# A wide weight conversion, a held first unit and held token-row weights in an RWKV-6 and MLP-mixer kernel

## The chip, the cores and the metric

One core of one Trainium2 chip. The metric is the device time of one execution in microseconds (us).

## The reference

```
attention:  state = 0
            for t: y[t] = r[t] . (state + u*k[t] (x) v[t]);  state = w[t]*state + k[t] (x) v[t]
            r,k,v,w: (4 batches, 8 heads, 768 tokens, 48), float32
mixer:      x = y as (4, 768, 384)
            u = x + (relu(x^T w_tok1) w_tok2)^T          w_tok1 (768,256), w_tok2 (256,768)
            out = u + relu(u w_ch1) w_ch2                w_ch1 (384,1536), w_ch2 (1536,384)
```

The four mixer weights arrive as 64-bit floats. The kernel loads their bits and makes 32-bit floats of them on VectorE.

## The kernel before

Twelve attention **units** (three for each batch, 256 tokens each) go through six levels: a product (`gram`) on TensorE, a **join** on VectorE that multiplies r and k by decays, and a pick of the product into a weight tile `at`. The mixer of batch b runs woven with the units of batch b+1. The profile names TensorE's products by their result: `h_ps` for the token products, `z_ps` for the products with `w_ch1`, `q_ps` for those with `w_ch2` (in the first part of batch 0 these are one long sum, also called `h_ps`, the "down product"). The framework puts each engine's instructions in an order of its own by estimated readiness, and an instruction that waited held its engine: in the trace of the kernel before, VectorE ran nothing in the 1.01 us before 200.14 us, for which L358, a row product shown below, waited for its load. A dependency of class NoSync only fixes which of two instructions of one engine is issued first. It added no wait: in experiment 10, where it ties each VectorE step of the conversion to the one before, the second mask step starts 0.33 us after the first, which takes 0.42; untied, in the kernel before, mask steps start 0.336 apart.

The conversion, two pieces of 128x512 a call, their steps alternating:

```
bits64 = [t[:, ts(i, 2 * PIECE)] for t in (scratch, spare) for i in range(2)]
...
def convert(pair, first):
    steps = []
    for n, (dst, src) in enumerate(pair):
        d64 = bits64[(first + n) % 4]
        sp.dma_start(d64..., src)
        ...
        steps.append([
            dve: e     = top & 0x7FF0                  # exponent
            act: power = Relu(8*e + rebias)
            dve: m     = hi & 0xFFFFF | 0x100000       # mantissa
            dve: mf    = lo * 2**-32 + m
            dve: mf    = mf * 2**-20 * power
            dve: dst   = hi & 0x80000000 | mf ])       # sign
    for both in zip(*steps):
        for f in both:
            f()
```

(The steps are abridged to one line each.) From unit 6 on, the weight of a token for itself and for its successor is made by rows on VectorE and then placed:

```
def row(c):
    ...
    dve.tensor_mul(rr, rr, k.unsqueeze(1).to_broadcast([128, 2, DM]))       # L357
    dve.tensor_mul(rr[:, 0], rr[:, 0], u_rows)                              # L358
    dve.tensor_reduce(out=sums[0][:, c], in_=..., op=ALU.add)               # L359
def place():  ...  dve.copy_predicated(out=weights_at[i % 3]..., ...)       # L370
...
return [(0.3, lambda: row(0)), (0.3, lambda: row(1)), (0.2, lambda: (place(), load_near(i + 1)))]
```

and unit i's products stand beside the levels of unit i+1 in this program order:

```
return [(1.0, begin[1]), tokens, one(carry, rest[0]), update, one(before, rest[1]), row0, one(within, rest[2]),
        *loads, row1, *rest[3:], place]
```

## Time and profile before

| | before |
|---|---|
| time, median of 6 runs | 609.95 us (608.86 to 610.78) |
| span of the profiled run | 607.9 us |
| TensorE busy | 578.5 us, 95% |
| VectorE busy | 362.6 us, 60%, in 685 instructions |
| ScalarE busy | 180.1 us, 30% |

TensorE's busy time is near the span, yet "busy" also counts products that run at half rate (from 227.59 us fourteen `q_ps` take 4.78 us, where the fastest steady rate, 0.1625 each, gives 2.3). The prediction therefore compares each window with the work in it at the fastest steady rate. I call the difference the **ledger's loss**, and use it throughout.

### The profile page before, as it was taken

To read this page: it belongs to the slowest core of one execution; us is meant where nothing else is said; L and a number is where in the kernel's file an instruction comes from. 1 tells how busy PE (TensorE), PEld (TensorE's weight loads), DVE (VectorE), ACT (ScalarE), POOL (GpSimd) and SP (SyncE) were. 2 spreads that over 40 slices of the span, in tenths; PEclk is the share of its full clock that TensorE was granted. 3 is DMA by queue.
4 is the path that set the end of the run, shared out by engine and by line. 5 is a ranking of instruction groups with operands and counts; after the bars stand their busy time and mean duration, and the time that the engine had idled before them with its cause. 6 is when DMAs were issued, how large, how long until landed. Compare 5 with 4: busy or idle time off the path is not lost.

```text
span 607.9 us, 18977 instructions
## 1 busy us (share of the span) xinstructions
PE 578.5 (95%) x8596; PEld 493.5 (81%) x8596; DVE 362.6 (60%) x685; ACT 180.1 (30%) x440; POOL 7.2 (1%) x32
## 2 busy tenths in 40 slices
PE   3889789999999989999999999999999999999997
PEld 2777467876988877689989897789899886898987
DVE  5888889998786998876545463526253432040403
ACT  6154655530433313143132222232212311303020
POOL 4000000000000000000000000000000000000000
PEclk9999779999999998999999999999999999999999
DMA  8326554630335364532112100000000000000000
GB/s 340 121 81 215 153 175 156 208 96 27 82 108 136 93 165 135 146 105 51 56 29 76 32 28 27 2 1 2 29 2 28 1 28 1 0 14 13 27 2 26
DMA packets 22976, 45.85 MB, mean 75 GB/s; under 512 B 2512, under 2 KB 14928, under 8 KB 22896
## 3 DMA queue, kind: packets, MB, share of 16 engines
q1 hardware_dynamic: 22752, 44.64, 23.6%
q8 instruction: 67, 1.10, 0.8%
q14 instruction: 13, 0.11, 0.1%
q10 hardware_dynamic: 144, 0.00, 0.0%
HBM read 39.91 MB, written 4.72 MB: 73 GB/s over the span
## 4 chain that ended last, share of the span: by engine, by line
PE 78%; DVE 15%; issue 2%; ACT 2%; DMA 2%; SPq 0%; DVEq 0%; ACTq 0%
PE z_ps L533 26%; PE q_ps L567 24%; PE gram L276 7%; PE h_ps L506 5%; PE h_ps L513 3%; PE h_ps L543 3%; PE kv_ps L413 2%; PE y_ps L468 2%; PE gram L403 2%; DVE rk L317 2%; PE y_ps L455 2%; DVE wch L192 1%; DVE sums L359 1%; DVE at L292 1%; PE gram L270 1%
## 5 line engine op out<-in xcount | busy, mean ns | idle before, releaser
L533 PE MATMUL z_ps<-xT,wch 128*128 128x256 f32 x864 | 195.6, 382 | 0.1
L533 PEld LDWEIGHTS z_ps<-xT,wch 128*128 128x128 f32 x864 | 161.0, 190 | 22.3 <-ACT z L535 1.4
L535 ACT ACTIVATE z<-z_ps 128x256 f32<-128x256 f32 x144 | 55.2, 383 | 167.3 <-PE z_ps L533 158.3
L567 PE MATMUL q_ps<-wch,z 128*128 128x192 f32 x528 | 97.5, 334 | 0.7 <-DVE o L589 0.7
L567 PEld LDWEIGHTS q_ps<-wch,z 128*128 128x128 f32 x528 | 88.3, 194 | 2.4 <-DVE o L589 1.0
L567 PE MATMUL q_ps<-scratch,z 128*128 128x192 f32 x396 | 70.2, 329 | 0.0
L276 PE MATMUL gram<-rk 48*64 48x32 f32 x3072 | 65.0, 239 | 4.4 <-DVE at L292 1.7
L276 PEld LDWEIGHTS gram<-rk 48*64 48x64 f32 x3072 | 60.6, 158 | 10.5 <-issue 3.8
L567 PEld LDWEIGHTS q_ps<-scratch,z 128*128 128x128 f32 x396 | 64.5, 190 | 0.6
L317 DVE TENSOR_TENSOR rk<-rk,w 112x1024 f32<-112x1024 f32 x27 | 32.8, 1222 | 30.5 <-PE gram L276 26.8
L317 DVE TENSOR_TENSOR rk<-rk,decay 112x1024 f32<-112x1024 f32 x27 | 33.0, 1222 | 27.1 <-PE gram L276 16.7
L559 DVE TENSOR_TENSOR z<-z 128x768 f32<-128x768 f32 x11 | 10.5, 956 | 61.0 <-ACT z L535 61.0
L506 PE MATMUL h_ps<-x,wtok 128*128 128x384 f32 x96 | 39.9, 561 | 1.8 <-ACT x L474 1.8
L513 PE MATMUL h_ps<-h,wtok 128*128 128x384 f32 x96 | 35.3, 492 | 0.0
L300 ACT COPY at<-gram 16x256 f32<-16x256 f32 x48 | 17.4, 364 | 58.5 <-PE gram L276 57.3
L292 DVE COPY_PREDICATED at<-mask,gram 128x512 f32<-128x512 uint8 x36 | 32.3, 897 | 0.0
L506 PEld LDWEIGHTS h_ps<-x,wtok 128*128 128x128 f32 x96 | 19.9, 220 | 13.1 <-issue 3.0
L515 DVE TENSOR_TENSOR x<-x,h_ps 128x384 f32<-128x384 f32 x24 | 13.3, 554 | 27.4 <-PE h_ps L513 27.3
L513 PEld LDWEIGHTS h_ps<-h,wtok 128*128 128x128 f32 x96 | 16.5, 190 | 9.5 <-ACT h L508 2.6
L287 ACT COPY at<-gram 32x256 f32<-32x256 f32 x48 | 17.4, 363 | 15.1 <-PE gram L270 14.6
L404 ACT COPY kT<-gram 128x512 f32<-128x512 f32 x24 | 14.1, 586 | 26.4 <-PE gram L403 26.2
L436 DVE TENSOR_TENSOR state<-state,kv_ps 128x192 f32<-128x192 f32 x30 | 10.7, 357 | 18.5 <-PE kv_ps L413 18.1
(90 smaller groups left out, 551.0 us busy)
## 6 DMA issues: line engine op xcount, KB each, us to landing
rk<-in_rkw_dram SPq DMA_DIRECT2D x36, 192.0 KB, 3.5
scratch<-in_w_ch_dram SPq DMA_DIRECT2D x10, 512.0 KB, 4.3
vt<-in_v_dram SPq DMA_DIRECT2D x12, 384.0 KB, 4.2
out_dram<-o SPq DMA_DIRECT2D x24, 192.0 KB, 1.9
rp<-in_near_dram SPq DMA_DIRECT2D x12, 384.0 KB, 3.5
x<-in_w_ch_dram SPq DMA_DIRECT2D x8, 512.0 KB, 4.2
w<-in_rkw_dram SPq DMA_DIRECT2D x18, 192.0 KB, 3.5
rk<-in_rkw_dram SPq DMA_DIRECT2D x6, 512.0 KB, 6.5
```

The costliest lines, as they stand in the source:

```text
L276: fours(lambda q, j, rows, cols: pe.matmul(g[cols, q, ts(ca, 32)], k_[rows, ds(ca * 128 + j * T, T)], right[rows, ts(2 * ca + j, 32 // b), ...
L287: act.copy(at[p:p + b, :, ts(c, A), b:], g[ds(p + c * b, b)])
L292: dve.copy_predicated(out=dst, data=g.rearrange("p q (m b) -> p q m b", b=b), mask=masks[l].rearrange("p x t -> p (x t)").rearrange("p (m ...
L300: act.copy(at[p:p + b, :, :, n * 2 * b + b:(n + 1) * 2 * b], g[p:p + b, :, :, ts(n, b)])
L317: dve.tensor_mul(halves, halves, by)
L404: act.copy(L["kT"][:, c], ps)
L506: pe.matmul(sums[i], wtok1[:, c, ts(i, 128)], xs[bt][:, c, :], start=(c == 0), stop=(c == C - 1))
L513: pe.matmul(ps, wtok2[:, i, ts(c, 128)], h1[:, i, :], start=(i == 0), stop=(i == DTOK // 128 - 1))
L533: pe.matmul(ps, wch1[:, m, ts(jt, 128)], xT[:, m, ts(s, SEG)], start=(m == 0), stop=(m == DM // 128 - 1))
L535: act.activation(zs[s][:, jt, :], ps, AF.Relu)
L543: pe.matmul(ps, zs[0][:, jt, ts(n, 128)], wch2[:, jt, :], start=(jt == 0), stop=(jt == NJ - 1))
L567: pe.matmul(ps, a[:, j, :], b[:, j, :], start=(j == 0), stop=(j == HJ - 1))
```

## The change

Three parts. The conversion handles both pieces of a call in one wide instruction a step, and its raw buffers alternate without a break from the token weights to the channel weights. The VectorE work of unit 3, beyond its first block, is issued after the last conversion. The token-row products go to the end of their unit in program order and are issued after whatever VectorE instruction was then the newest.

```
+    def newest(engine):
+        return next(ins.name for ins in reversed(block.instructions) if ins.engine == engine.engine)
+    def late(mark, engine, f):
+        done = len(block.instructions)
+        f()
+        for ins in block.instructions[done:]:
+            if ins.engine == engine.engine:
+                tc.add_manual_dep(ins, mark, no_sync, reason="order of issue")
...
-    bits64 = [t[:, ts(i, 2 * PIECE)] for t in (scratch, spare) for i in range(2)]
+    bits64 = [t[:, :4 * PIECE] for t in (scratch, spare)]
...
-        for both in zip(*steps):
-            for f in both:
-                f()
+        dve.tensor_scalar(e, top, 0x7FF0, None, op0=ALU.bitwise_and)
+        act.activation(power, e, AF.Relu, bias=rebias, scale=8.0)
+        dve.tensor_scalar(m, hi, 0xFFFFF, 0x100000, op0=ALU.bitwise_and, op1=ALU.bitwise_or)
+        dve.scalar_tensor_tensor(mf, lo, 2.0 ** -32, m, op0=ALU.mult, op1=ALU.add)
+        dve.scalar_tensor_tensor(mf, mf, 2.0 ** -20, power.bitcast(bf16), op0=ALU.mult, op1=ALU.mult)
+        for n, (dst, src) in enumerate(pair):
+            ...  dve.scalar_tensor_tensor(dst.bitcast(u32), sign, 0x80000000, x, ...)
...
-        return [(0.3, lambda: row(0)), (0.3, lambda: row(1)), (0.2, lambda: (place(), load_near(i + 1)))]
+        return [(0.3, lambda c=c: late(newest(dve), dve, lambda: row(c))) for c in range(UC)] + [
+            (0.2, lambda: (place(), load_near(i + 1)))]
...
-        return [(1.0, begin[1]), tokens, one(carry, rest[0]), update, one(before, rest[1]), row0, one(within, rest[2]),
-                *loads, row1, *rest[3:], place]
+        return [(1.0, begin[1]), tokens, one(carry, rest[0]), update, one(before, rest[1]), one(within, rest[2]),
+                *loads, *rest[3:], row0, row1, place]
...
-    to_ch = conversion((wch1, w_ch1, 1, 512), (wch2, w_ch2, 4, 128))
+    to_ch = conversion((wch1, w_ch1, 1, 512), (wch2, w_ch2, 4, 128), first=2)
...
+            converted = newest(dve)
...
-            att = levels(n) if bt == 0 else []
+            att = []
+            if bt == 0:
+                begin, first, *rest = levels(n)
+                att = [begin, first] + [(c, lambda f=f: late(converted, dve, f)) for c, f in rest]
```

(The parity instructions of the rows now use `late` too, with the same marks as before.)

More of the change, by code (lines that the diff above doesn't have):

```diff
@@ L164, in rwkv6_then_mixer @@
     scratch = wide.tile([128, 8 * PIECE], u32, name="scratch")
-    bits64 = [t[:, ts(i, 2 * PIECE)] for t in (scratch, spare) for i in range(2)]
-    mantissas = [scratch[:, ts(i, PIECE)] for i in (4, 5)]
-    exponents = [scratch[:, ts(i, PIECE)].bitcast(u16).rearrange("p (two n) -> p two n", two=2) for i in (6, 7)]
+    bits64 = [t[:, :4 * PIECE] for t in (scratch, spare)]
+    mantissas = scratch[:, ts(2, 2 * PIECE)]
+    exponents = scratch[:, ts(3, 2 * PIECE)].bitcast(u16).rearrange("p (two n) -> p two n", two=2)
     rebias = const.tile([128, 1], f32, name="rebias")
@@ L171, in convert @@
     def convert(pair, first):
-        steps = []
+        d64 = bits64[first // 2 % 2]
         for n, (dst, src) in enumerate(pair):
-            d64 = bits64[(first + n) % 4]
-            sp.dma_start(d64.rearrange("p (c k) -> p c k", c=dst.shape[1]), src)
-            lo, hi = (d64.rearrange("p (n two) -> p n two", two=2)[:, :, j] for j in range(2))
-            top = d64.bitcast(u16).rearrange("p (n four) -> p n four", four=4)[:, :, 3]
-            m, mf = mantissas[n], mantissas[n].bitcast(f32)
-            e, power = exponents[n][:, 0], exponents[n][:, 1]
-            steps.append([
-                lambda top=top, e=e: dve.tensor_scalar(e, top, 0x7FF0, None, op0=ALU.bitwise_and),
-                lambda e=e, power=power: act.activation(power, e, AF.Relu, bias=rebias, scale=8.0),
-                lambda hi=hi, m=m: dve.tensor_scalar(m, hi, 0xFFFFF, 0x100000, op0=ALU.bitwise_and, op1=ALU.bitwise_or),
-                lambda lo=lo, m=m, mf=mf: dve.scalar_tensor_tensor(mf, lo, 2.0 ** -32, m, op0=ALU.mult, op1=ALU.add),
-                lambda mf=mf, power=power: dve.scalar_tensor_tensor(mf, mf, 2.0 ** -20, power.bitcast(bf16),
-                                                                    op0=ALU.mult, op1=ALU.mult),
-                lambda hi=hi, m=m, dst=dst: dve.scalar_tensor_tensor(
-                    dst.bitcast(u32), hi.rearrange("p (c k) -> p c k", c=dst.shape[1]), 0x80000000,
-                    m.rearrange("p (c k) -> p c k", c=dst.shape[1]), op0=ALU.bitwise_and, op1=ALU.bitwise_or)])
@@ L195, in convert @@
-        for both in zip(*steps):
-            for f in both:
-                f()
+            sp.dma_start(d64[:, ts(n, 2 * PIECE)].rearrange("p (c k) -> p c k", c=dst.shape[1]), src)
+        lo, hi = (d64.rearrange("p (n two) -> p n two", two=2)[:, :, j] for j in range(2))
+        top = d64.bitcast(u16).rearrange("p (n four) -> p n four", four=4)[:, :, 3]
+        m, mf = mantissas, mantissas.bitcast(f32)
+        e, power = exponents[:, 0], exponents[:, 1]
+        dve.tensor_scalar(e, top, 0x7FF0, None, op0=ALU.bitwise_and)
@@ new lines, in convert @@
+        act.activation(power, e, AF.Relu, bias=rebias, scale=8.0)
[3 more added lines that the diff above has]
+        for n, (dst, src) in enumerate(pair):
+            sign, x = (t[:, ts(n, PIECE)].rearrange("p (c k) -> p c k", c=dst.shape[1]) for t in (hi, m))
+            dve.scalar_tensor_tensor(dst.bitcast(u32), sign, 0x80000000, x, op0=ALU.bitwise_and, op1=ALU.bitwise_or)
@@ L203, in blocks, with conversion @@
         return [(t[:, ds(i, c), ds(j, k)], bits[:, ds(i, c), ds(2 * j, 2 * k)]) for i, j in (sorted(at) if c == 4 else at)]
-    def conversion(*weights):
+    def conversion(*weights, first=0):
         pieces = [e for w in weights for e in blocks(*w)]
-        return [(0.2, lambda n=n: convert(pieces[n:n + 2], n)) for n in range(0, len(pieces), 2)]
+        return [(0.2, lambda n=n: convert(pieces[n:n + 2], first + n)) for n in range(0, len(pieces), 2)]
     xs = {}
@@ L373, in place, with parities @@
                 mask=masks[0].rearrange("p x (m two) -> p x m two", two=2).to_broadcast([128, 2 * UC * A, T // 2, 2]))
-        return [(0.3, lambda: row(0)), (0.3, lambda: row(1)), (0.2, lambda: (place(), load_near(i + 1)))]
+        return [(0.3, lambda c=c: late(newest(dve), dve, lambda: row(c))) for c in range(UC)] + [
+            (0.2, lambda: (place(), load_near(i + 1)))]
     near_by = {}
     def begin_near():
-        marks = [next(ins.name for ins in reversed(block.instructions) if ins.engine == e.engine) for e in (dve, sp)]
-        for mark, ins in zip((marks[0], marks[0], marks[1]), (
-                dve.tensor_reduce(out=odd, in_=parity, axis=mybir.AxisListType.X, op=ALU.add),
-                dve.tensor_scalar(odd, odd, -1.0, 1.0, op0=ALU.mult, op1=ALU.add),
-                sp.dma_start(u_rows, u_all))):
-            tc.add_manual_dep(ins.ins, mark, no_sync, reason="not in the first batch's way")
+        def parities():
+            dve.tensor_reduce(out=odd, in_=parity, axis=mybir.AxisListType.X, op=ALU.add)
+            dve.tensor_scalar(odd, odd, -1.0, 1.0, op0=ALU.mult, op1=ALU.add)
+        late(newest(dve), dve, parities)
+        late(newest(sp), sp, lambda: sp.dma_start(u_rows, u_all))
         load_near(NEAR)
```

## The prediction

> **What bounds the kernel now.** I read, in order, the page, the busy time by window, the chain of waits, and the timelines of VectorE and TensorE. The page's part 2 comes first (40 slices of 15.2 us).
>
> ```profile
> PE   3889789999999989999999999999999999999997
> DVE  5888889998786998876545463526253432040403
> PEclk9999779999999998999999999999999999999999
> ```
>
> TensorE is the bound over most of the span. The granted clock dips twice: at slices 4 and 5 (61 to 91 us) and at slice 15 (228 to 243 us). VectorE is full in slices 6 to 8 and again in 13 and 14. The busy time by window shows the same in us. Its columns are window, length, then busy time with count for PE, PEld, DVE, ACT, POOL, then clock, DMA share and GB/s.
>
> ```profile
> 60.00:80.00 20.00, 16.02 (x390) 10.63 (x388) 16.11 (x37) 10.87 (x25) 0.00 (x0) 0.83 0.54 147
> ...
> 100.00:120.00 20.00, 20.00 (x95) 17.06 (x93) 20.00 (x42) 10.50 (x25) 0.00 (x0) 1.00 0.58 186
> ...
> 200.00:220.00 20.00, 18.25 (x322) 16.43 (x323) 19.82 (x38) 5.17 (x13) 0.11 (x1) 1.00 0.37 101
> 220.00:240.00 20.00, 18.35 (x425) 15.04 (x424) 17.61 (x31) 5.57 (x14) 0.00 (x0) 0.83 0.55 160
> 240.00:260.00 20.00, 19.65 (x304) 13.21 (x303) 17.45 (x35) 4.06 (x10) 0.11 (x1) 1.00 0.48 139
> ```
>
> "Busy" flatters TensorE, so I made a ledger: products in a window, each at its fastest steady rate in this trace, against the window's length. The rates come from the chain: z_ps 72 in 15.54 us (0.216 each), q_ps 84 in 13.65 (0.1625), the 384-wide h_ps 0.323, a batch of 64 small gram products about 1.0. **Lost time** by this ledger: 49.5 us before 100, 2.9 from 100 to 200, 8.1 from 200 to 260, under 1 from 260 to 500. So what the change can win lies before 100 us or between 200 and 260 us. In 100 to 147 us, where the weights are converted, VectorE is 100% busy, yet 95 z_ps products in 20 us are 20.5 us at the peak rate: TensorE is the bound there too.
>
> The chain of waits between 185 and 262 us (start, us, what) says what costs the 8 us:
>
> ```profile
> 196.49 3.63 DMA u_rows<-in_u_all_dram
> 200.12 0.02 issue
> 200.14 1.03 DVE rp L358 x2
> ...
> 223.03 0.88 DVE rp L357
> 223.91 0.02 issue
> 223.93 0.56 DVE rp L358
> 224.49 1.15 DVE rk L317
> 225.68 1.91 PE gram L276 x64
> 227.59 4.78 PE q_ps L567 x14
> ```
>
> L357 to L359 are the token-row weights. They stand in front of L317, the join that the next gram needs. When that gram comes, it and the q_ps after it run at half rate: 14 q_ps in 4.78 us, where 14 times 0.1625 is 2.3.
>
> [...]L358 at 200.14 waited 1.01 us for the u_rows load, and nothing behind it ran.[...] The trace has the half rate (q_ps 0.34 against 0.1625), after idle pieces of 0.7, 1.4 and 0.2 us within six[...].[...]
>
> **The change part by part.**
>
> *Wide conversion.* One pair of pieces before, by the VectorE timeline (start, duration of the two, line):
>
> ```profile
> 113.59 0.74 DVE L186 TENSOR_SCALAR scratch<-x 128x512 uint16<-128x512 uint16 x2
> 114.26 0.74 DVE L188 TENSOR_SCALAR scratch<-x 128x512 uint32<-128x512 uint32 x2
> 114.94 1.27 DVE L189 SCALAR_TENSOR_TENSOR scratch<-x,scratch 128x512 f32<-128x512 uint32 x2
> 116.14 1.28 DVE L190 SCALAR_TENSOR_TENSOR scratch<-scratch 128x512 f32<-128x512 f32 x2
> 117.34 1.28 DVE L192 SCALAR_TENSOR_TENSOR wch<-x,scratch 128x512 uint32<-128x512 uint32 x2
> 118.55 0.74 DVE L186 TENSOR_SCALAR scratch<-scratch 128x512 uint16<-128x512 uint16 x2
> ```
>
> Starts are 4.96 us apart: four steps of 0.336 and six of 0.603.[...] The change makes four of the ten instructions disappear: two wide steps of 0.603, two of about 1.137 (L317, as wide, steps by 1.13 to 1.14), two final ones of 0.603. Sum 4.69, so 0.27 less a pair and 3.3 us of VectorE over twelve pairs. One wide ACT instruction of about 1.15 us replaces two of 0.72; the two VectorE steps that hide it last 1.74. Nearly all of the 3.3 us lies beside full TensorE work. Only some three and a half pairs run before 100 us, about 1.0 us of VectorE, and VectorE idles 7 us between 38 and 86: I credit **0.5 us** on the path.
>
> *Alternating raw buffers.* Before, the last token-weight pair and the first channel-weight pair both use scratch. The second one's load goes out at 77.88, after the first one's end at 75.7, and its conversion starts at 83.64. With the other buffer it can be loaded at about 66, and VectorE has idle pieces of 2.0, 1.9 and 1.5 us near 69, 77 and 91 to run it in. The conversions should end some 4 to 6 us sooner than 133.68. TensorE has its z_ps and h_ps of 100 to 147 to do in any case, so this gives slack to the second batch's first unit and little time: **0.5 us**.
>
> *The hold.* Only the order of issue is constrained, no data wait added. In the timeline before, unit 3's first join and picks run at 75 to 85 and its next join at 133.68, directly behind the last conversion. The hold keeps what is already so: **0**.
>
> *Token-row weights.* Twelve L357 exist, two a unit for units 6 to 11. They start at 190, 192, 213, 219, 223, 227, 236, 246, 255, 259, 263 and 266. But the placements (L370), which use them, come at 238.25, 278.58 and 324.54. So rows of five later units are made in front of unit 6's neighbours, when VectorE has least time. One row steps 0.87 + 0.47 + 0.87 = 2.2 us. Eight rows in 200 to 260 are not due, 17.6 us of the 54.9 that VectorE is busy there. Taken away, the busy share is 37 of 60, 62%, like the 14.2 and 9.9 us of 20 found in 280 to 320, where TensorE loses nothing. The u_rows load also gets time to land. The 8.1 us lost should shrink to 1 or 2: **6.5 us** won. The rows come back later, some 6 us a unit, in stretches where VectorE is about half idle; I charge **0.5 us** for that.
>
> Sum: 0.5 + 0.5 + 0 + 6.5 - 0.5 = 7 us. 609.7 - 7 = 602.7; since the clock could also stay up longer before 91 us, I say **602**.
>
> **The rivals.** *The row cluster becomes a new wait.* Two rows and a placement are about 6.3 us on VectorE in one piece, at the last levels of a unit, before the next unit's join and the weighted products of its own values. For it: in the q_ps stages VectorE also has four z sums of 0.87 each. Against it: a unit takes over 30 us in later batches. If each of six units lost 1 us, gain falls to 1 or 2 us and the time is about 608. *The loads become the bound of the conversion.* A wide step needs both 512 KB pieces at once; landing takes a median of 4.2 to 4.3 us, and one piece came 0.19 us late already at 124. With a period of 4.69 instead of 4.96 the gain in VectorE time may vanish; this stays under full TensorE work, so about 603. *The clock decides before 91 us.* Eight h_ps at 86.26 take 4.30 us where the peak needs 2.6.[...] *A held level chain starves TensorE after the conversion*, if the units then wait on one engine: 606 to 610. It speaks against this that the order before is the same.
>
> **Range and chances.** The rows' 6.5 us is the main term, with an uncertainty of about 3; the clock before 91 us gives another 3 either way. So 595.5 to 608. Faster by over 2% needs under 597.5, both terms at their best: 0.13. Slower by over 2% needs over 622, for which no mechanism above is large enough: 0.02. The rest, 0.85, is within 2%.
>
> **What would show the steps right or wrong.** Conversion pairs start about 4.7 us apart and count six VectorE instructions. L357 starts come in pairs, each pair shortly before its placement and not all by 267 us. The clock in slice 15 is back to 9, and the ledger's loss from 200 to 260 is under 3 us. VectorE busy there falls from 54.9 to about 37 us. If the loss moves to the stretch after 260 instead, the first rival is right. If the stretch before 100 us changes by more than 2 us, my credit for the conversion was mis-sized. If the windows from 200 to 260 still lose 6 us or more with rows gone, the joins and not the rows were the bound.

## The result, and the profile after

604.86 us, median of 6 runs (603.08 to 608.32), against 609.95 us. The ratio is 0.992, with a 95% interval of 0.989 to 0.9949. A ratio is the mean time of one kernel's fast runs over that of the other's of the same rounds, so it is not quite the ratio of the medians.

The profiled run (span 606.6 us) was the slowest of the six. This matters below. Part 2 of its page:

```profile
PE   3888789999999989999999999999999999999997
DVE  5888787999685768665557467527456432040404
PEclk9995689999999999999999999999999999999999
```

The clock dip at slice 15 is gone, and VectorE is no longer full at slices 13 and 14. The early dip is there; in this run it is deeper and starts a slice sooner than before (slices 3 to 5, counted from 0, show 5, 6 and 8, where slices 4 and 5 showed 7 and 7). The busy time by window after, for the three windows that lost 8.1 us:

```profile
200.00:220.00 20.00, 19.51 (x385) 17.52 (x386) 15.29 (x27) 6.14 (x16) 0.11 (x1) 1.00 0.25 72
220.00:240.00 20.00, 18.21 (x440) 14.53 (x439) 15.95 (x27) 5.68 (x15) 0.00 (x0) 1.00 0.31 92
240.00:260.00 20.00, 19.65 (x304) 13.71 (x303) 12.62 (x26) 4.44 (x11) 0.11 (x1) 1.00 0.35 90
```

VectorE's busy time fell from 54.9 to 43.9 us, and the ledger's loss from 8.1 to 4.4 us. The clock is full in all three; before, it was 0.83 in the mean from 220 to 240 us (0.50 from 225.7 to 232.4), and the missing 0.17 of 20 us is 3.4 us (an estimate from these figures, as TensorE was busy there for 18.35 of the 20 us). By this estimate most of what the rows cost was paid as half rate, and only a smaller part as idle time. The chain of waits after, at the place where the rows stood in front of a join (in the changed kernel the join is L323, the gram L282, the q_ps L575):

```profile
223.37 1.23 DVE rk L323
...
225.82 1.14 PE gram L282 x64
226.95 2.15 PE q_ps L575 x12
```

The gram takes 1.14 us where it took 1.91, and twelve q_ps take 2.15 us where fourteen took 4.78. No row stands in this stretch of the chain. The rows have become L363 to L365 and the placement L376. In the timeline of VectorE:

```profile
234.75 0.95 DVE L363 TENSOR_TENSOR rp<-rp,kp 128x768 f32<-128x768 f32 x1
...
237.88 0.95 DVE L363 TENSOR_TENSOR rp<-rp,kp 128x768 f32<-128x768 f32 x1
...
241.06 1.31 DVE L376 COPY_PREDICATED at<-mask,two 128x1024 f32<-128x1024 uint8 x1
...
265.36 0.96 DVE L363 TENSOR_TENSOR rp<-rp,kp 128x768 f32<-128x768 f32 x1
267.96 0.95 DVE L363 TENSOR_TENSOR rp<-rp,kp 128x768 f32<-128x768 f32 x1
```

Each unit's two rows now stand in front of their own placement. The conversion is the surprise. One wide pair in the full stretch:

```profile
112.44 0.69 DVE L196 TENSOR_SCALAR scratch<-x 128x1024 uint16<-128x1024 uint16 x1
113.05 0.69 DVE L198 TENSOR_SCALAR scratch<-x 128x1024 uint32<-128x1024 uint32 x1
113.77 1.23 DVE L199 SCALAR_TENSOR_TENSOR scratch<-x,scratch 128x1024 f32<-128x1024 uint32 x1
115.10 1.23 DVE L200 SCALAR_TENSOR_TENSOR scratch<-scratch 128x1024 f32<-128x1024 f32 x1
116.36 1.29 DVE L203 SCALAR_TENSOR_TENSOR wch<-x,scratch 128x512 uint32<-128x512 uint32 x2
117.57 0.69 DVE L196 TENSOR_SCALAR scratch<-scratch 128x1024 uint16<-128x1024 uint16 x1
```

The durations are as I had reckoned; the starts are not. From L196 to L198 it is 0.61 us, an overlap of 0.08. But L199 starts 0.72 after L198, L200 1.33 after L199, and L203 1.26 after L200: the whole duration and a little more. A pair takes 5.13 us, where the narrow one took 4.96. Six instructions are slower than ten.

To see where the time went without the spread of the early stretch, I cut each profiled run at three events. They are the first product with channel weights (z_ps), the first down product (h_ps<-wch), and the first token product of batch 1 (h_ps<-x). "Down to end" is the time from the second of them to the end of the span.

| kernel | first z_ps at | down to end | loss, down to batch 1 |
|---|---|---|---|
| before | 100.03 | 475.6 | 11.3 |
| after, first trace | 102.16 | 471.2 | 6.6 |

The gain from the first down product on is 4.4 us. The first trace lost 2.1 us before z_ps and 1.0 between z_ps and down. Whether that belongs to the change or to that run, the experiments had to say; experiment 12 does.

### The profile page after: what moved, and what is told of

It is laid out like the page before. It is cut to its first block, busy times and chain, and to the rows that moved or that the text cites.

```text
span 606.6 us, 18914 instructions
## 1 busy us (share of the span) xinstructions
PE 575.0 (95%) x8596; PEld 490.0 (81%) x8596; DVE 362.8 (60%) x637; ACT 177.4 (29%) x428; POOL 7.2 (1%) x32
## 4 chain that ended last, share of the span: by engine, by line
PE 82%; DVE 12%; issue 2%; ACT 2%; DMA 2%; SPq 0%; DVEq 0%; ACTq 0%
PE z_ps L541 28%; PE q_ps L575 24%; PE gram L282 8%; PE h_ps L514 6%; PE h_ps L521 3%; PE h_ps L551 3%; PE kv_ps L421 2%; PE y_ps L463 2%; PE gram L411 2%; PE y_ps L476 2%; DVE scratch L200 1%; DVE scratch L199 1%; DVE at L298 1%; DVE rk L318 1%; DVE rk L323 1%
## 5 line engine op out<-in xcount | busy, mean ns | idle before, releaser
L575 PE MATMUL q_ps<-wch,z 128*128 128x192 f32 x528 | 94.9, 329 | 0.0
L575 PEld LDWEIGHTS q_ps<-wch,z 128*128 128x128 f32 x528 | 86.1, 190 | 1.3
L575 PE MATMUL q_ps<-scratch,z 128*128 128x192 f32 x396 | 69.8, 328 | 0.0
L282 PE MATMUL gram<-rk 48*64 48x32 f32 x3072 | 64.1, 235 | 6.0 <-issue 2.1
L282 PEld LDWEIGHTS gram<-rk 48*64 48x64 f32 x3072 | 59.3, 154 | 12.5 <-issue 6.2
L575 PEld LDWEIGHTS q_ps<-scratch,z 128*128 128x128 f32 x396 | 64.5, 190 | 0.4
L323 DVE TENSOR_TENSOR rk<-rk,decay 112x1024 f32<-112x1024 f32 x27 | 33.0, 1223 | 31.4 <-PE gram L282 23.0
L323 DVE TENSOR_TENSOR rk<-rk,w 112x1024 f32<-112x1024 f32 x27 | 32.9, 1223 | 27.9 <-PE gram L282 21.7
L293 ACT COPY at<-gram 32x256 f32<-32x256 f32 x48 | 17.4, 364 | 14.9 <-PE gram L276 14.5
```

What stands on the lines that cost most here:

```text
L282: fours(lambda q, j, rows, cols: pe.matmul(g[cols, q, ts(ca, 32)], k_[rows, ds(ca * 128 + j * T, T)], right[rows, ts(2 * ca + j, 32 // b), ...
L293: act.copy(at[p:p + b, :, ts(c, A), b:], g[ds(p + c * b, b)])
L323: dve.tensor_mul(halves, halves, by)
L575: pe.matmul(ps, a[:, j, :], b[:, j, :], start=(j == 0), stop=(j == HJ - 1))
```

## The experiments

Theory after the result: the hold of the rows is the whole gain, and the conversion gives nothing, because each wide step waits for the step right in front of it. Rivals: that the wide form pays before 100 us, that the hold of unit 3 matters, or that the place of the rows in program order does the work.

Summary (medians in us; before is between 608.6 and 609.6 in all these rounds):

| run | time | ratio, 95% interval | first z_ps at | down to end | loss, down to batch 1 |
|---|---|---|---|---|---|
| 1 rows_only | 606.34 | 0.9943 (0.9917 to 0.9970) | 101.89 | 470.5 | 6.2 |
| 2 wide_only | 607.93 | 0.9998 (0.9968 to 1.0027) | 102.98 | 475.6 | 11.2 |
| 3 all_but_wide | 607.04 | 0.9973 (0.9950 to 0.9995) | 98.01 | 473.1 | 8.1 |
| 4 no_hold | 604.43 | 0.9927 (0.9906 to 0.9947) | 99.27 | 470.3 | 6.5 |
| 5 rows_moved | 609.48 | 1.0006 (0.9986 to 1.0025) | 100.67 | 474.2 | 10.0 |
| 6 rows_late | 604.96 | 0.9924 (0.9901 to 0.9947) | 100.42 | 471.0 | 6.3 |
| 7 no_rows (wrong) | 611.15 | 1.0044 (1.0008 to 1.0080) | 100.23 | 474.1 | 9.9 |
| 8 small_rows (wrong) | 605.79 | 0.9938 (0.9915 to 0.9961) | 98.88 | 470.7 | 6.1 |
| 9 half_wide | 611.17 | 1.0025 (1.0004 to 1.0046) | 104.78 | 472.5 | 7.1 |
| 10 serial_narrow | 613.34, one run | none | 99.20 | 479.0 | 14.9 |
| 11 half_ordered | 609.25 | 1.0000 (0.9974 to 1.0025) | 102.85 | 472.1 | 7.3 |
| 12 after_again | 604.93 | 0.9931 (0.9907 to 0.9955) | 97.42 | 471.1 | 7.1 |

### 1. The row change alone (rows_only)

The kernel before with the third part of the diff and the helper functions, nothing else.

> The kernel before with the third part alone (row products moved to the end of their unit and held in order of issue). Theory: the rows made too early cost nearly all of the 8 us lost between 200 and 260 us, and they are the whole gain. Then about 604.5 to 606 us, a loss from 200 to 260 us of 3 to 5 us by the ledger, L357-type starts in pairs near their placements. Rival: the gain comes from the conversion or the hold; then 608.5 to 610 us and the loss in that stretch stays near 8.

606.34 us, just outside the expected times, with the loss in the stretch as expected. From the first down product on it takes 470.5 us, as little as the whole change. Rows alone give the later gain.

### 2. The conversion alone (wide_only)

The kernel before with the first part of the diff: wide steps and alternating buffers.

> The kernel before with the wide conversion and the alternating raw buffers, without hold or row change. Theory: a wide step must wait for the step right in front of it, where the narrow pair has another piece's step between; a pair takes about 5.13 us in the full stretch (as in the trace after) against 4.96, so no gain: 609 to 613 us. Rival, my prediction: fewer instructions free VectorE and win about 1 us: 608 to 609.5 us, period under 4.9.

No difference: 0.9998. The median of 607.93 is lower than expected, that of before in the same rounds is 609.12, and the interval takes in 1. The period is 5.12 us again, not the rival's 4.9 or less, and the time from down to end is that of before to a tenth.

### 3. All but the wide form (all_but_wide)

```
 (the changed kernel, with bits64, mantissas, exponents and convert() of before; first=2, the hold and the rows kept)
```

> The changed kernel with the narrow conversion of before put back (buffers alternating throughout, hold and row change kept). Theory: the wide form costs 1 to 3 us before 135 us, so this is faster than the changed kernel: 601.5 to 604 us, against before 0.987 to 0.991, period of a pair 4.96 us. Rival: the wide form wins about 1 us as predicted; then 605.5 to 607 us.

A miss for my theory: 607.04, not 601.5 to 604. The narrow pair does take 4.96 us here, yet the kernel is no faster. In the VectorE timeline unit 3's first picks stand at 129.59 and 131.46, behind the conversions. In the changed kernel they stand at 83.48, long before. A gram batch, 1.06 us of TensorE work, moved behind the first down product with them. The loss there is 8.1 instead of 6.6. So the shorter period won nothing that could be seen, and a different order, which the framework chose for the narrow steps, cost more. That the order is the cause of the difference in time is argued from this trace, not shown by a run of its own; the same form without the hold of unit 3 was not run either. The run shows one thing more: with narrow steps and alternating buffers the last conversion ends at 128.40 us, 5.4 us sooner than the 133.76 of the kernel before.

### 4. Without the hold of unit 3 (no_hold)

```
-                att = [begin, first] + [(c, lambda f=f: late(converted, dve, f)) for c, f in rest]
+                att = [begin, first] + rest
```

> The changed kernel without the hold. My prediction gave the hold 0: then 604 to 606 us, as with it. Rival: without it the second batch's level work is put in front of the conversions, which then end later, and TensorE waits for channel weights: 607 us or more, with the last conversion ending 3 us or more later than 139 us.

604.43 us (603.74 to 605.4) lies inside the range of the changed kernel. The hold gives nothing that the medians show with the rest of the change in place, as predicted. The reason given for that did not hold: without it the next pick of unit 3 after its first block stands at 86.45 us, with it at 143.47 and 138.86 in the two traces, so in the wide form the hold does change the order. From the first z_ps to the end the one trace without it takes 502.8 us, the two with it 504.4 and 504.2; one trace against two is no proof that the hold costs something. It was not tried with the wide form alone.

### 5 and 6. Place or hold of the rows (rows_moved, rows_late)

Experiment 5 changes only the program order of `row0` and `row1`. Experiment 6 leaves that order and adds only `late(newest(dve), dve, ...)` around each row.

> The kernel before with the row products only moved to the end of their unit in program order, not held. Theory: the scheduler lifts work that looks ready over what stands in front of it, so the move alone leaves rows made early; the loss between the first channel product of the second kind and the next batch's token products (11.3 us before, 6.2 with the whole row change) stays above 9 us, time 608 to 610 us. Rival: the place in program order is what counts; then the loss falls to about 6.5 us and the time to 604.5 to 606.5 us.

> The kernel before with the row products held in order of issue at their old place in program order. Theory: the hold ends the early rows, though they now stand in the middle of the unit; the loss in the same stretch falls to 6 to 8 us, time 604.5 to 607 us. Rival: a row held in mid unit stands in front of the joins; loss stays above 9 us, 608 to 611 us.

The move alone: 1.0006, nothing in the total. In its timeline the twelve row products still start between 190.5 and 266.6 us, as they did before, because the framework lifts them to the front again. The hold alone: 0.9924, the whole gain. Its rows start at 219.08, 229.66, 254.34, 263.48, 298.80 and 307.47, two to each placement. The window from 220 to 240 us, first with the move alone, then with the hold alone:

```profile
220.00:240.00 20.00, 18.12 (x432) 14.90 (x433) 19.20 (x34) 5.57 (x14) 0.11 (x1) 0.91 0.54 160
```

```profile
220.00:240.00 20.00, 18.95 (x367) 14.40 (x359) 15.22 (x28) 6.33 (x16) 0.00 (x0) 1.00 0.53 157
```

VectorE is busy for 19.2 of 20 us and the clock dips with the move; 15.2 us and full clock with the hold. In its one trace the move takes 1.4 us less from down to end than before (474.2 for 475.6). Its clock dip is smaller, 0.91 for 0.83 in this window, by the same estimate 1.8 us lost for 3.4, which accounts for about that much. The four traces with early rows (before, wide_only, rows_moved and serial_narrow) show a dip between 220 and 240 us, the ten with held or removed rows show none: fourteen q_ps in a row take 4.85, 4.85, 3.79 and 4.22 us in the four, 0.27 to 0.35 each, and every group of six or more q_ps in the ten takes 0.18 to 0.19 each.

### 7 and 8. What rows still cost (no_rows, small_rows)

Both give a wrong result. Experiment 7 puts a memset of the sums in place of a row's three instructions. Experiment 8 puts one multiplication of 16 elements there that reads both tiles of the row.

> Wrong on purpose: the changed kernel with each row's three VectorE instructions replaced by one small memset of its sums. Theory: after the change rows cost next to nothing on the path; the loss in the same stretch stays at 5.5 to 6.6 us and the time within 1.5 us of the changed kernel, 603 to 605.5 us. Rival: rows still hold up the joins at the end of their unit; then loss falls under 5 us and the time under 602.5 us.

611.15 us: less work, and slower than the kernel before. The waits of VectorE between 185 and 238 us show why:

```profile
DVE rk L323 <- DMA rk<-in_rkw_dram: 5.0, 1, 5.0
```

With nothing to read the row buffers, their loads are issued in a bunch: 18 (rp and kp) from 185 to 215 us, where the changed kernel has 3. The next unit's operand, whose load is issued at 196.5 us among them, lands at 201 us, 5 us after VectorE was ready to join. TensorE's next gram waits 2.6 us for that join, near the 2.9 us by which this trace is longer than the changed kernel's from down to end (474.1 for 471.2). The medians differ by 6.3 us, and this trace does not show where the rest goes. This run answers another question than it was meant to, so it was mended:

> Wrong on purpose, in place of the run without rows, whose unread loads came early and held up the next unit's operands: the changed kernel with each row's three VectorE instructions replaced by one that reads 16 elements of both its tiles, so that the buffers come free where they did. Theory: held rows cost little on the path; from the first down product to the end the changed kernel takes 471.1 us, this 470 to 471.2, the time 603 to 605.5 us. Rival: rows hold up the joins also at their new place; then under 469 us and under 602.5 us.

605.79 us at the median, a little over what was expected, but the trace settles it: 470.7 us from down to the end against 471.1, and a loss of 6.1 against 6.6 to 7.1. VectorE's busy time from 200 to 260 us fell further, from 43.9 to 38.3 us, and half a microsecond came of it. The rows at their new place cost next to nothing. What is still lost there was not taken apart. The idle pieces of TensorE that its trace names between 200 and 260 us are short, the longest 0.6 us behind the state and 0.5 us behind a join, so the level chain (gram to join to gram) is a guess.

### 9, 10 and 11. Why the wide pair takes 5.13 us (half_wide, serial_narrow, half_ordered)

Experiment 10 takes the kernel before and puts the steps of one piece one behind the other:

```
-        for both in zip(*steps):
-            for f in both:
-                f()
+        for one in steps:
+            for f in one:
+                ... f(), with the order of issue fixed behind the last step ...
```

> The kernel before with the narrow steps of one piece put one behind the other instead of alternating with the other piece's. Same ten instructions a pair, same widths. Theory of the exposed wait: each dependent step starts only after the whole duration of the one in front plus some 0.03 to 0.1 us, as in the wide form's trace: 0.336 + 0.445 + 0.78 + 0.71 + 0.603 = 2.87 us a piece, 5.75 us a pair against 4.96. Rival: distance does not matter and the wide form's period comes from elsewhere; then the period stays at 4.95 to 5.05 us.

Same ten instructions, same widths. One piece in its VectorE timeline:

```profile
108.61 0.42 DVE L188 TENSOR_SCALAR scratch<-x 128x512 uint16<-128x512 uint16 x1
108.94 0.42 DVE L190 TENSOR_SCALAR scratch<-x 128x512 uint32<-128x512 uint32 x1
109.40 0.69 DVE L191 SCALAR_TENSOR_TENSOR scratch<-x,scratch 128x512 f32<-128x512 uint32 x1
110.20 0.69 DVE L192 SCALAR_TENSOR_TENSOR scratch<-scratch 128x512 f32<-128x512 f32 x1
110.92 0.69 DVE L194 SCALAR_TENSOR_TENSOR wch<-x,scratch 128x512 uint32<-128x512 uint32 x1
111.53 0.42 DVE L188 TENSOR_SCALAR scratch<-x 128x512 uint16<-128x512 uint16 x1
```

A piece takes 2.92 us and a pair 5.84, expected 5.75, against 4.96 when they alternate. The gaps are those of the wide form: 0.46 for 0.34 behind the mantissa mask, 0.80 and 0.72 for 0.60 behind the two sum steps. What a step waits for is the step right in front of it, and another piece's step between them hides that.

Experiment 9 keeps the two mask steps wide and halves the three later ones, without the hold of unit 3; experiment 11 fixes its order besides.

```
-        dve.tensor_scalar(e, top, ...); act.activation(power, e, ...); dve.tensor_scalar(m, hi, ...)
-        dve.scalar_tensor_tensor(mf, lo, ...); dve.scalar_tensor_tensor(mf, mf, ...)
+        dve.tensor_scalar(m, hi, ...); dve.tensor_scalar(e, top, ...)
+        for h in half: act.activation(power[:, h], e[:, h], ...)
+        for h in half: dve.scalar_tensor_tensor(mf[:, h], lo[:, h], ...)
+        for h in half: dve.scalar_tensor_tensor(mf[:, h], mf[:, h], ...)
```

> The changed kernel without the hold, and the conversion with only the two mask steps wide, the three later steps in two halves that alternate, so that no step waits for the one right in front of it. Theory of the exposed wait: two starts of 0.603 and six of 0.603, a period of about 4.83 us in the full stretch, against 5.12 wide and 4.96 narrow; the total stays within noise of the wide form, 603 to 605.5 us, as TensorE is the bound there. Rival: the period of the wide form is set by the loads or by ScalarE; then it stays at 5.0 or more.

The time, 611.17 us, is a miss. The period of 5.2 to 6.0 us from 115 us on looks like another, with a gap of 0.25 to 1.06 us between the mask's end and the sum step. But that gap is no wait: the VectorE timeline shows steps of unit 3, which is not held here, standing in it.

```profile
105.31 0.68 DVE L196 TENSOR_SCALAR scratch<-scratch 128x1024 uint32<-128x1024 uint32 x1
...
110.13 0.68 DVE L197 TENSOR_SCALAR scratch<-x 128x1024 uint16<-128x1024 uint16 x1
...
116.11 0.68 DVE L196 TENSOR_SCALAR scratch<-scratch 128x1024 uint32<-128x1024 uint32 x1
116.72 1.22 DVE L327 TENSOR_TENSOR rk<-rk,w 112x1024 f32<-112x1024 f32 x1
117.85 1.28 DVE L202 SCALAR_TENSOR_TENSOR scratch<-scratch 128x512 f32<-128x512 uint32 x2
```

The pair from 105.31 to 110.13 has no foreign step in it and takes 4.82 us. The three from 115.50 on take 5.96, 5.42 and 5.15, and less the foreign steps (1.14, 0.60 and 0.34 from start to start) each is 4.82: the theory's 4.83. So the period is a hit, and the miss is in the time alone. The text of the next experiment was recorded before this was seen and still names an unknown wait.

> The form with two wide mask steps and halved later steps, with its order fixed (mantissa mask, exponent mask, then the halves in turn), as the scheduler had put the mantissa mask right in front of the step that needs it. Theory of the exposed wait: eight starts of 0.603, a period of 4.83 us in the full stretch, the shortest of all forms. Rival: something else holds the first sum step (0.25 to 1.06 us in the unordered form); then the period stays above 5.0. In either case total within 2 us of the other forms with held rows, 603 to 608 us.

With the order fixed, the steps that the theory covers start 0.60 to 0.62 apart, but a pair takes 4.94 us, not 4.83. The extra 0.12 stands in one place:

```profile
128.62 1.29 DVE L208 SCALAR_TENSOR_TENSOR wch<-scratch 128x512 uint32<-128x512 uint32 x2
129.95 0.69 DVE L197 TENSOR_SCALAR scratch<-x 128x1024 uint32<-128x1024 uint32 x1
130.56 0.69 DVE L198 TENSOR_SCALAR scratch<-x 128x1024 uint16<-128x1024 uint16 x1
```

L208 is two instructions of 0.60, yet L197 starts 1.33 after them. L197 overwrites the mantissas that the last L208 reads, and it now comes first. The wait moved from a read behind a write to a write behind a read. In the pair from 114.89 on, another unit's step of 0.34 stands between the two; it takes 5.17, again 4.83 and the foreign step. The total, 609.25 us, is outside the expected range and no better than before. Both half forms lose 16 to 18 us between 62 us and the first z_ps, where before loses 12.8. That each form's order in that crowded stretch weighs more than its period is a guess: the first z_ps stands at 104.78 and 102.85 in their traces, and the changed kernel's own two traces have it at 102.16 and 97.42. Against no_hold the half forms are about 5 and 7 us slower by the medians, of which 2 lie after the first down product (472.1 and 472.5 for 470.3). What costs them was not taken apart.

### 12. The changed kernel again (after_again)

> The changed kernel once more, for a second trace and its spread. Theory: what differs between its runs is the stretch before the first channel product (102.2 us in the first trace, its slowest run); from the first down product on the time is the same as in the first trace, 471.2 us, within 0.6. Times 603 to 606 us. Rival: the spread comes from the later stretches.

604.93 us, 603.38 to 607.09. The second trace starts z_ps at 97.42 where the first started it at 102.16, with the same program. From down to the end the two take 471.1 and 471.2 us. So the spread of the changed kernel is made before the first channel product. In the first 62 us alone the ledger's loss is 35.9 in one and 38.4 in the other. All traces taken have 35.9 to 36.5 or 37.8 to 38.8 there, two groups. TensorE's clock record differs in the same stretch (0.70 from 40 to 60 us in the first trace, 0.83 in the second), but I did not control it, so the cause is not shown.

The 1.0 us between the first z_ps and down is another matter: both traces of the changed kernel take 33.2 us there, before takes 32.3, so it belongs to the change. In both, z_ps waits once for 0.92 us. The chain of waits in the first trace:

```profile
122.69 0.70 DVE scratch L196
...
123.47 1.15 ACT scratch L197
124.62 0.28 ACT z L543
124.90 0.04 issue
124.95 2.21 PE z_ps L541 x9
```

ScalarE stands idle for 1.61 us until the exponent mask is there, then makes its wide step of 1.15 us, and the z that TensorE waits for comes behind it. In this stretch every trace with the wide form and no halves has such a wait of 0.7 to 1.0 us; the longest in the traces with narrow steps or halves is 0.32. Without the hold (no_hold, wide_only) the stretch still takes only 32.5 and 32.4 us; why the loss shows only with the hold is not known. It is over before the first down product, so the column "down to end" does not see it.

No version beats the changed kernel beyond the noise. Without the hold it is at 604.43; with nothing but `late` around the rows it is at 604.96.

## Why the prediction was right, and where its sums were not

The time (604.86) lies in the range and, at 0.8% below before, within the 2% to which the prediction gave 0.85. The mechanism of the main term holds: rows made too early stood in front of the joins, and the late gram and the q_ps behind it ran at half rate (clock 0.50 from 225.7 to 232.4 us; the gram took 1.91 us, 1.14 after). That the time came within 3 us of 602 is in part luck: the rows gave less than forecast, and the spread of the early stretch, 4.7 us between two traces of one program, is as large as the gain. Point by point:

- **Rows, 6.5 us less 0.5.** Right in kind, too large. Measured from the first down product on: 4.4 us for the whole change, 4.6 for the hold of rows alone. The rows left the window nearly as forecast: their three instructions kept VectorE busy for 20.5 us from 200 to 260 us before (26 instructions) and for 4.8 after (6 instructions), 15.7 us less, against 17.6. But other VectorE work moved into the room, two more joins (13 for 11) among it, and the busy time fell by 11.0 us to 43.9, not to 37. The mis-sized term is the 6.5 us: the loss was to shrink to 1 or 2 us and shrank to 4.4. Most of the rest was not the rows', as the run with tiny rows shows: VectorE down to 38.3 us there, and half a microsecond won.
- **Why they came early.** I described program order and hold as one term. The runs split it: the move is worth nothing in the time, the hold the whole gain.
- **Wide conversion, 0.5 us.** The sum of 4.69 us a pair failed. It took the start-to-start step of instructions that do not depend on each other and used it for a chain in which each does. The three dependent steps add 0.12, 0.19 and 0.12, and 4.69 becomes 5.12. (Its 1.137 is the step of L317 in the trace, 1.13 to 1.14 us for 1024 elements; its 0.603 for a wide mask was the author's estimate, and L196 to L198 take 0.61.) For the time it is worth nothing alone (0.9998), as TensorE is nearly the bound in that stretch (busy 20.00 of 20 us from 100 to 120 us before), which the prediction said. What it missed is ScalarE: the wide exponent step was to be hidden, and it held up z_ps for 0.7 to 1.0 us. One reading was off too: five pairs start before 100 us in the kernel before, and a sixth at 97.78, not three and a half.
- **Alternating buffers, 0.5 us.** The conversions were to end 4 to 6 us sooner than 133.68. With narrow steps they did: experiment 3 ends them at 128.40, 5.4 us sooner. With the wide form the last one ends at 139.3 in the first trace and 134.7 in the second, and at 140.5 in wide_only, so with the wide form nothing of it is left. In time it won nothing in either form. The alternation by itself was not run; rows_late, which differs from experiment 3 in it, in the hold and in the place of the rows, ends at 134.1.
- **The hold, 0.** Right by the medians, but not because it keeps the order: see experiment 4.
- **The clock.** Slice 15 is back at 9, as predicted. The chance that the early dip would change was put at plus or minus 3 us, the author's estimate, and what sets that dip was not shown; the two traces of one program differ by 4.7 us there.
- **Rivals.** The row cluster did not become a wait: from batch 1's token products to the end the changed kernel takes 372.9 us against 374.0. The loads held the wide conversion once, 0.60 us at 105.92, and did not set its period.

## What to carry to other kernels

When an off-path engine's work is ready early and a scheduler takes it early, look at what stands behind it in the same engine's queue: fixing the order of issue was worth 5 us here, moving it in the program nothing. The price of a short delay can be paid later, as half rate: an estimated 3.4 us of it here, after idle pieces of TensorE of 0.71, 1.43 and 0.21 us between 218 and 226 us. Before merging two narrow chains into a wide one, count the steps that depend on the one right in front; the alternation of two chains was hiding that wait, and ten alternating instructions (4.96 us) beat six dependent ones (5.13). Look also at the queue of the engine that gets the wider step: what stands behind it can wait longer (here z_ps for 0.7 to 1.0 us behind the wide exponent step, at most 0.32 otherwise). When a gap between two steps seems to have no reason, list everything that ran on the engine in that gap. And removing work can hurt when that work was pacing the release of buffers and with it the loads: without the rows one load held VectorE for 5.0 us.
